# Second readings of the weights after attention: one landing tile or three, and how many pieces between two examinations

## The chip, the cores and the metric

The kernel runs on one core of one Trainium2 chip. The metric is device time in microseconds (us), the median of three runs, for the whole program: attention, the feed-forward block and all reading and writing of memory.

## The reference

Two computations follow each other. The first is a gated linear recurrence over 4 batches, 8 heads, 768 time steps and a head width of 48:

```python
for t in range(S):
    state = alpha[:, :, t, :, None] * state + np.einsum('bhd,bhe->bhde', k[:, :, t], v[:, :, t])
    y[:, :, t] = np.einsum('bhd,bhde->bhe', q[:, :, t], state)
```

The heads are then laid side by side (3072 tokens of width 384), and a feed-forward block is applied: `h = x @ w_in` (384 x 2048), `g = h * sigmoid(h)`, `out = g @ w_out` (2048 x 384). The weights come as 64-bit floats, everything else as 32-bit floats.

## The kernel before

Attention is cut into 24 chunks of 128 steps (one batch each), which go through the stages `products`, `quotient`, `scores`, `values` and `states`. From chunk 8 on, a chunk's alpha, k and q land in three fixed tiles, `late["quads"]` with the names a, k and q, each 128 x 800 floats. VectorE (DVE) turns them (`turned`), and each is free again once that has read it.

The feed-forward block works on groups of four chunks (six groups, `grp` 0 to 5). A group's first product goes into `g` tiles, and its second product goes out to memory. Both use fast-product schemes that trade matmuls for sums on DVE. They are written as Python generators, and one step of a generator is a *piece*. For a group from 2 on:

- `enter(grp, pair)` makes half of the hidden units in seven pieces, called E1 to E7 here. A piece has three products of two matmuls each (E7 has two products), into three PSUM banks `ps_m`; the profile records each matmul as two. ScalarE (ACT) copies a bank away or DVE adds or subtracts it (`tt`, recorded at line 944). DVE has one such step in each of E1 to E4, three in E5, four in E6, and three in E7, one of them recorded at L587. E7 also ends with two `side_by_side` sums (L1019). The activation (L941) is on ACT.
- `leave(grp, h)` makes the output for half a group's tokens in seven pieces, L1 to L7 here. Each is one product of eight matmuls (16 records) into one of the two banks `ps_o`, which `new(0)` and `new(1)` take. A line number with an L, such as L1042, is always four digits or three; L1 to L7 are pieces. L1 and L7 both take bank 0. L7's bank is emptied by DVE in `store` (line 1042), which also starts the write of the output. `subtract` (L1033) is DVE work, twice in each of L1, L3 and L4.

The list `pieces` fixes the order. After attention there are 41 pieces left: the rest of a *first block* (`leave(4,0)` and `enter(5,0)` in turn, L1 E1 L2 E2 ... L7 E7), a *second block* (`leave(4,1)` and `enter(5,1)`), and a *tail* (`leave(5,0)`, then `leave(5,1)`, L1 to L7 each with nothing between). `go_on()` issues the next piece.

The kernel is right only for inputs within certain bounds, and so it examines its inputs: the generator `audit()` reads alpha, w_in and w_out a second time, in 9, 12 and 16 transfers. DVE reduces each one, by one maximum for alpha and by a maximum and a minimum for the weights (line 685). Every transfer lands in the one tile `bits` of the pool `look`, so the next cannot start before the reduction is over. During attention's late steps `fill` takes a step of `audit()` every second slot. After attention a loop takes the remaining 17 steps, with one or two pieces after each in turn:

```python
    while next(audits, 0) is None:
        turns += 1
        for _ in range(1 + turns % 2):
            go_on()
```

After the loop DVE works out the flag: four reductions and comparisons (`ends`, `good`), five pieces, then one small matmul on TensorE (PE) and its comparison (`small`, line 1236), four pieces, then `values_load` (line 1239), with which each engine's sequencer reads the flag from memory. A hint for the branch at the program's end follows on each engine, then all pieces left. If the flag is zero a slower general version runs.

The framework's planner puts the instructions of each engine into one fixed order: by program order where inputs are ready by its own estimates, and with a later instruction ahead of an earlier one where they are not. `keep_in_program_order` ties an instruction behind the one traced just before it on its engine. It is used for every matmul in this phase and for the audit's reductions. It is not used for `tt`, `subtract` and `store`, nor for the flag's own steps. Each engine then runs its order strictly. The audit's transfers are issued by SyncE's queue (SP). So are the tail's outputs, while the outputs of earlier groups go by GpSimd's queue (POOL).

Of the kernel before, what the change touches and what calls it, by code (L numbers as in the profile page):

```python
# [8 lines left out]
F32 = mybir.dt.float32  # L9
I32 = mybir.dt.int32  # L10
# [345 lines left out]
def quotients(  # L356
# [19 lines left out]
    nc = tc.nc  # L376
    dve, act, gps = nc.vector, nc.scalar, nc.gpsimd

    late = {}
# [14 lines left out]
    B, H, S, D = q.shape  # L394
    C = 128
    NCH = S // C
    NP = H // 2
    HD = H * D
# [174 lines left out]
    quads = w_in.rearrange("p k (q i c) -> p i k q c", i=4, c=128)  # L573
# [83 lines left out]
    def audit():  # L657


        flat = alpha.rearrange("b h s d -> (b h s d)").rearrange("(p c) -> p c", p=128)  # L660
        todo = [(flat[:, c : c + AW], AW, 0) for c in range(0, flat.shape[1], AW)]
        if wide:
            todo += [(moe_w_in[t * 128 : t * 128 + 128, c : c + 512], 512, 1)
                     for c in range(0, DF, 512) for t in range(NKT)]
            todo += [(moe_w_out[f * 128 : f * 128 + 128, :], HD, 1) for f in range(NFT)]
        for kind in (0, 1):
            n = sum(x[2] == kind for x in todo)
            if n:
                seen.append([fix.tile([128, n], F32, name=f"seen{kind}{i}") for i in range(2)])
        at = [0, 0]  # L670
        for src, n, kind in todo:
            t = late["look"].tile([128, 512, 2], I32, name="bits")
            if kind == 0:
                x = t.rearrange("p n w -> p (n w)")[:, 0:n].bitcast(F32)
                nc.sync.dma_start(x, src)
            else:
                nc.sync.dma_start(t[:, 0:n, :].rearrange("p n w -> p (n w)"), src.bitcast(I32))
                x = t[:, 0:n, 1]
            yield
            i = at[kind]  # L680
            at[kind] += 1
            for which, op in ((0, ALU.max), (1, ALU.min)):
                if kind == 1 or which == 0:
                    tc.keep_in_program_order(
                        dve.tensor_reduce(seen[kind][which][:, i : i + 1], x, axis=AX, op=op,  # L685
                                          apply_absolute_value=True))
# [454 lines left out]
    def go_on():  # L1141

        nonlocal done
        next(pieces[done][0], None)
        done += 1

    audits = audit()
    done, bridged = 0, 0
    STEPS = NT + 1
# [4 lines left out]
    def settle():  # L1154

        first.close()
        late.update(look=pool("look"), part=pool("part"), xc=pool("xc"), turn=pool("turn"),
                    wx=pool("wx").tile([128, 8, NQ, 128], F32, name="wx"))
        quads = pool("quads")
        late["p"] = pool("p").tile([128, NP * W + 1], F32, name="p")  # L1160
        late["quads"] = {name: quads.tile([128, 32 + 4 * NP * D], F32, name=f"{name}t") for name in "akq"}
        for name, t in late["quads"].items():
            gps.memset(t, 1.0 if name == "a" else 0.0)
        load(NA)
# [20 lines left out]
    for step in range(STEPS):  # L1185
# [9 lines left out]
        for slot, group in enumerate(stages):  # L1195
            for stage, lag in group:
                n = step - lag
# [9 lines left out]
            if step * SLOTS + slot == (NA + 1) * SLOTS - 1:  # L1207
                x = decayed.rearrange("p (o i c) -> p o i c", o=2, c=C)
# [2 lines left out]
            fill(step, slot)  # L1211
            if step * SLOTS + slot >= NA * SLOTS - 1 and conv_done[1] == NFT and not late:
                settle()
    turns = 0
    while next(audits, 0) is None:
        turns += 1
        for _ in range(1 + turns % 2):
            go_on()

    checks = [(least.rearrange("p n j -> p (n j)"), ALU.min, 2.0**-64, ALU.is_gt),  # L1220
              (seen[0][0], ALU.max, 1.0, ALU.is_le)]
# [27 lines left out]
@with_exitstack  # L1249
def kernel(  # L1250
    ctx: ExitStack,
    tc: tile.TileContext,
    q: bass.AP,
    k: bass.AP,
    v: bass.AP,
    alpha: bass.AP,
    moe_w_in: bass.AP,
    moe_w_out: bass.AP,
    out: bass.AP,
):  # L1260


    flag = ctx.enter_context(tc.tile_pool(name="flag", bufs=1))
    small = flag.tile([1, 1], I32, name="small")
    args = (q, k, v, alpha, moe_w_in, moe_w_out, out)
    within = quotients(tc, small, *args)
    with tc.If(within < 1, label="general"):
        general(tc, *args)
# [30 lines left out]
```

## Time and profile before

| What | Value |
| --- | --- |
| median of 3 runs | 561.12 us (560.93 to 561.14) |
| span of the profiled execution, first to last instruction | 558.1 us |
| around the span, median less span | 3.0 us |
| PE busy | 541.4 us (97%) |
| DVE busy | 445.1 us (80%) |
| ACT busy | 208.4 us (37%) |
| POOL busy | 75.9 us (14%) |
| mean granted TensorE clock | 0.994 |
| DVE, line 685 (the audit): busy, idle before it | 42.5 us, 24.0 us |
| matmul pieces of attention end at about | 443 us |
| audit transfers of w_out issued | 454.2 to 514.8 us |

The profiled execution's own time is not listed apart from its span; the 3.0 us around it are what the runs have beyond the span. A group of instructions is one row: busy time, mean length of one in nanoseconds, and the idle time of its engine just before, with what ended it. Starts in a timeline are in us from the start of the span, and the second figure is the length of the row's instructions together. Ends of matmuls are modelled, so distances between starts are the safer measure on PE.

### The profile page before, as it was taken

What the parts mean: (1) busy time and instruction counts of PE and PEld (TensorE: products, weight loads), DVE (VectorE), ACT (ScalarE), POOL (GpSimd) and SP (SyncE); (2) the same over time, 40 slices, a digit from 0 to 9 for tenths busy, and PEclk for the clock granted to TensorE, in tenths of its full rate; (3) what the DMA queues carried; (4) which work ended last, traced back from release to release, by engine and by line L of the source; (5) the groups of instructions that cost most, each with busy time, mean ns of one, the idle gap of its engine ahead of it and who ended that gap; (6) DMA issues with size and microseconds to landing.
All of it is one profiled execution on the core that took longest, in us unless ns stands there. A gap on an engine that the chain in (4) does not pass through costs nothing. (4 is left out here: it accounts for less than half of the span.)

```text
span 558.1 us, 12640 instructions
## 1 busy us (share of the span) xinstructions
PE 541.4 (97%) x5026; PEld 488.8 (88%) x5026; DVE 445.1 (80%) x801; ACT 208.4 (37%) x466; POOL 75.9 (14%) x146
## 2 busy tenths in 40 slices
PE   5999999999999999999999999999999999999996
PEld 3788887998899898899999999988998999998996
DVE  5887889974999799997998986998894775857531
ACT  3456643223333243353353353353263341432200
POOL 4100010221211211021021021021121000001000
PEclk9799999999999999999999999999999999999999
DMA  9999861164445525355445654717712122333101
GB/s 218 255 276 177 232 189 40 38 164 108 126 131 136 142 62 134 88 145 157 129 109 142 194 141 115 198 22 179 180 48 84 53 99 95 111 109 106 38 25 32
DMA packets 99220, 70.13 MB, mean 126 GB/s; under 512 B 56272, under 2 KB 88656, under 8 KB 99152
## 3 DMA queue, kind: packets, MB, share of 16 engines
q1 hardware_dynamic: 97232, 65.30, 44.6%
q0 software_dynamic: 1920, 3.93, 2.0%
q8 instruction: 41, 0.67, 0.5%
q14 instruction: 27, 0.22, 0.1%
HBM read 61.34 MB, written 7.86 MB: 124 GB/s over the span
## 5 line engine op out<-in xcount | busy, mean ns | idle before, releaser
L388 PE MATMUL ps_o<-w_out,g 128*128 128x192 f32 x768 | 134.7, 329 | 1.1 <-DVE o L1042 0.9
L388 PEld LDWEIGHTS ps_o<-w_out,g 128*128 128x128 f32 x768 | 125.4, 190 | 5.1 <-DVE o L1042 2.3
L388 PE MATMUL ps_m<-xt,w_in 128*128 128x256 f32 x480 | 113.6, 383 | 1.5 <-ACT xt L851 1.1
L388 PEld LDWEIGHTS ps_m<-xt,w_in 128*128 128x128 f32 x480 | 89.1, 190 | 14.4 <-ACT xt L851 1.6
L388 PE MATMUL ps_o<-wt,g 128*128 128x192 f32 x576 | 99.7, 326 | 0.0
L388 PEld LDWEIGHTS ps_o<-wt,g 128*128 128x128 f32 x576 | 95.1, 190 | 1.6 <-issue 0.2
L388 PE MATMUL ps_m<-xc,w_in 128*128 128x256 f32 x288 | 70.7, 382 | 0.0
L685 DVE TENSOR_REDUCE seen<-bits 128x1 f32<-128x384 int32 (+2 forms) x65 | 42.5, 689 | 24.0 <-DMA bits<-in_moe_w_out_dram 19.6
L388 PEld LDWEIGHTS ps_m<-xc,w_in 128*128 128x128 f32 x288 | 53.6, 190 | 7.0 <-DVE g L944 0.3
L941 ACT ACTIVATE g<-g 128x1024 f32<-128x1024 f32 x32 | 33.0, 1056 | 59.0 <-DVE g L944 59.0
L1033 DVE TENSOR_TENSOR g<-g 128x512 f32<-128x512 f32 x72 | 49.8, 708 | 6.1 <-PE ps_o L388 6.1
L1045 POOL DMA_DIRECT2D out_dram<-o x40 | 22.0, 550 | 223.2 <-DVE o L1042 127.6
L813 POOL TENSOR_SCALAR_AFFINE_SELECT g<-g 64x256 f32<-64x256 f32 x64 | 34.2, 534 | 124.8 <-ACT g L806 105.8
L388 PE MATMUL ps_m<-xc,wx 128*128 128x256 f32 x192 | 50.0, 383 | 1.0 <-DVE xc L586 1.0
L936 ACT COPY g<-ps_m 128x512 f32<-128x512 f32 x64 | 36.5, 588 | 36.5 <-PE ps_m L388 36.4
L388 PEld LDWEIGHTS ps_m<-xc,wx 128*128 128x128 f32 x192 | 35.2, 190 | 5.3 <-ACT u L1064 1.3
L944 DVE TENSOR_TENSOR g<-ps_m,g 128x512 f32<-128x512 f32 x56 | 37.0, 684 | 2.9 <-PE ps_m L388 2.7
L722 DVE TENSOR_TENSOR_SCAN u<-al,one 128x516 f32<-128x516 f32 x24 | 30.0, 1249 | 10.6 <-ACT al L719 10.3
L909 ACT ACTIVATE g<-ps_m 128x512 f32<-128x512 f32 x32 | 19.1, 596 | 42.8 <-PE ps_m L388 42.3
L936 ACT COPY part<-ps_m 128x512 f32<-128x512 f32 x32 | 18.9, 589 | 43.0 <-DVE g L944 21.3
L752 DVE TENSOR_TENSOR_SCAN p<-al,inv 128x516 f32<-128x516 f32 x24 | 29.9, 1246 | 1.0 <-PE ps_a L388 0.4
L388 PE MATMUL ps_a<-g,vn 128*32 128x128 f32 x768 | 27.5, 278 | 1.8 <-POOL g L801 1.7
(126 smaller groups left out, 611.4 us busy)
## 6 DMA issues: line engine op xcount, KB each, us to landing
bits<-in_moe_w_in_dram SPq DMA_DIRECT2D x24, 512.0 KB, 4.8
bits<-in_moe_w_out_dram SPq DMA_DIRECT2D x32, 384.0 KB, 3.1
at<-in_alpha_dram SPq DMA_DIRECT2D x64, 96.0 KB, 2.5
kt<-in_k_dram SPq DMA_DIRECT2D x64, 96.0 KB, 2.5
qt<-in_q_dram SPq DMA_DIRECT2D x64, 96.0 KB, 2.6
bits<-in_alpha_dram SPq DMA_DIRECT2D x9, 512.0 KB, 3.8
out_dram<-o POOLq DMA_DIRECT2D x40, 96.0 KB, 2.4
flips<-turn SPq DMA_DIRECT2D x12, 256.0 KB, 2.4
```

What stands on the lines that cost most here:

```text
L388: in_order(nc.tensor.matmul(*args, **kw))
L685: dve.tensor_reduce(seen[kind][which][:, i : i + 1], x, axis=AX, op=op, apply_absolute_value=True))
L722: dve.tensor_tensor_scan(u[:, end - 1 :: -1], sg[:, end:0:-1], one[:, end:0:-1], 0.0, ALU.mult, ALU.add)
L752: dve.tensor_tensor_scan(p[:, 0:end], sg[:, 0:end], iv[:, 0:end], 0.0, ALU.mult, ALU.add)
L813: gps.affine_select(x, x, pattern=[[0, NP], [1, CH]], compare_op=ALU.is_ge, fill=0.0, base=0, channel_multiplier=-1)
L909: act.activation(gts[grp, h, pair][:, i : i + 2, q % 2, :], ps, AF.Silu)
L936: act.copy(to, ps)
L941: act.activation(x, x, AF.Silu)
L944: dve.tensor_tensor(to, a, b, op)
L1033: dve.tensor_tensor(cells(grp, h, pair, *to), cells(grp, h, pair, *x), cells(grp, h, pair, *y), ALU.subtract)
L1045: (gps if grp < NG - 1 else nc.sync).dma_start(out[r : r + C, c * HO : (c + 1) * HO], o)
```

## The change

`audit()` is split into a part that starts a transfer (`begin`) and a part that examines one. Transfers of alpha and w_in, 21 in all, still use the tile `bits`, one at a time. The 16 of w_out, which are 768 words wide, now land in the tiles a, k and q of attention in turn. From transfer number 20 on (counted from 0), up to two transfers beyond the one about to be examined are started. After attention the loop takes one piece per step of the audit, 17 in all, where it took two and one in turn, 26 in all. The flag's steps keep their distances of five and four pieces, and so they stand nine pieces earlier, as does all that follows them.

```diff
         flat = alpha.rearrange("b h s d -> (b h s d)").rearrange("(p c) -> p c", p=128)
+        assert 2 * HD <= 32 + 4 * NP * D
...
+        alone = sum(2 * x[1] > 32 + 4 * NP * D or x[2] == 0 for x in todo)
...
         at = [0, 0]
-        for src, n, kind in todo:
-            t = late["look"].tile([128, 512, 2], I32, name="bits")
+        landed = []
+
+        def begin(src, n, kind):
+            at = len(landed)
+            t = late["look"].tile([128, 512, 2], I32, name="bits").rearrange("p n w -> p (n w)") if (
+                at < alone) else late["quads"]["akq"[at % 3]].bitcast(I32)
             if kind == 0:
-                x = t.rearrange("p n w -> p (n w)")[:, 0:n].bitcast(F32)
-                nc.sync.dma_start(x, src)
+                landed.append(t[:, 0:n].bitcast(F32))
+                nc.sync.dma_start(landed[-1], src)
             else:
-                nc.sync.dma_start(t[:, 0:n, :].rearrange("p n w -> p (n w)"), src.bitcast(I32))
-                x = t[:, 0:n, 1]
+                nc.sync.dma_start(t[:, 0 : 2 * n], src.bitcast(I32))
+                landed.append(t[:, 0 : 2 * n].rearrange("p (n w) -> p n w", w=2)[:, :, 1])
+
+        for i, (src, n, kind) in enumerate(todo):
+
+            while len(landed) < min(i + (1 if i + 1 < alone else 3), len(todo)):
+                begin(*todo[len(landed)])
+            x = landed[i]
             yield
...
-    turns = 0
     while next(audits, 0) is None:
-        turns += 1
-        for _ in range(1 + turns % 2):
-            go_on()
+        go_on()
```

## The prediction

> **What bounds the kernel now.** I read the page's busy shares first (PE 97%), then the costliest groups for the audit, then PE's waits after attention, then the timelines around those waits. In the page's groups the audit is one row:
>
> ```profile
> L685 DVE TENSOR_REDUCE seen<-bits 128x1 f32<-128x384 int32 (+2 forms) x65 | 42.5, 689 | 24.0 <-DMA bits<-in_moe_w_out_dram 19.6
> ```
>
> DVE stood 24.0 us before reductions, 19.6 of them for transfers of w_out. That is no gain in itself. The waits that end on PE and on its weight loads (PEld) from 440 us on are few; these two lists hold all of substance:
>
> ```profile
> PE ps_o L388 <- DVE o L1042: 0.9, 2, 0.7
> ...
> PEld ps_o L388 <- DVE o L1042: 2.1, 3, 1.1
> PEld ps_a L388 <- issue: 0.6, 2, 0.3
> PEld ps_o L388 <- ACT g L941: 0.4, 1, 0.4
> ```
>
> So PE waits for `store` (L1042) and once for an activation. Where? The timeline of all engines at the end of the second block:
>
> ```profile
> 509.64 1.01 DVE L685 TENSOR_REDUCE seen<-bits 128x1 f32<-128x384 int32 x2 [0.91 <-DMA bits<-in_moe_w_out_dram]
> ...
> 510.48 2.76 PE L388 MATMUL ps_o<-wt,g 128*128 128x192 f32 x16
> ...
> 513.08 1.03 PE L388 MATMUL ps_m<-xc,w_in 128*128 128x256 f32 x4
> ...
> 513.75 1.00 DVE L685 TENSOR_REDUCE seen<-bits 128x1 f32<-128x384 int32 x2
> ...
> 513.94 1.03 PE L388 MATMUL ps_m<-xt,w_in 128*128 128x256 f32 x4
> 514.67 0.68 DVE L587 SCALAR_TENSOR_TENSOR g<-g 128x512 f32<-128x512 f32 x1
> 515.27 0.35 DVE L1042 TENSOR_TENSOR o<-ps_o,u 128x192 f32<-128x192 f32 x1
> ...
> 515.68 3.25 PE L388 MATMUL ps_o<-w_out,g 128*128 128x192 f32 x16 [0.71 <-DVE o L1042]
> ...
> 517.36 1.27 PEld L388 LDWEIGHTS ps_o<-w_out,g 128*128 128x128 f32 x8 [0.41 <-ACT g L941]
> ...
> 518.77 2.76 PE L388 MATMUL ps_o<-wt,g 128*128 128x192 f32 x16
> ```
>
> L7's product starts at 510.48 and is over at 513.08, but DVE, busy without a gap since 509.64 after 0.91 us lost to a transfer, comes to L7's `store` only at 515.27. The tail's L1 needs that bank.
>
> Undisturbed spacing: a four-record product takes 513.94 - 513.08 = 0.86, an L piece 2.60 (518.77 to 521.37, the next start). L1 was due at 513.94 + 0.87 = 514.81 and the piece behind it at 517.41, yet that starts at 518.77: **1.36 us lost** in the second block. The first block's end, from PE's own timeline:
>
> ```profile
> 477.27 1.03 PE L388 MATMUL ps_m<-xc,w_in 128*128 128x256 f32 x4
> 478.14 1.03 PE L388 MATMUL ps_m<-xt,w_in 128*128 128x256 f32 x4
> 479.24 2.87 PE L388 MATMUL ps_o<-w_out,g 128*128 128x192 f32 x16
> 481.94 1.89 PE L388 MATMUL ps_m<-xc,w_in 128*128 128x256 f32 x8
> ```
>
> The piece at 481.94 was due at 477.27 + 1.73 + 2.60 = 481.60: **0.34 us lost**. Everything else between 444 and 519 us runs at 2.60 a piece. What the change can win is thus 1.70 us.
>
> **The Trainium skill.** "PSUM — Partial Sum Buffer", Engine vs sequencer instructions: VectorE's queue is strictly first in, first out, and matmuls complete in program order. The trace agrees: at 515.27 `store` stood 2.2 us behind its product. "DMA: Bandwidth & Descriptors", Anatomy of one DMA: about 2.0 us fixed plus bytes / 436 GB/s, written for GpSimd's path; as an estimate 2.0 + 393,216 B / 436e3 = 2.9 us. SP's transfers of w_out show a median of 2.9 after 454 us, so it fits. "SBUF — State Buffer", Who interferes with whom: transfers don't contend with compute engines, nor `tensor_reduce` with GpSimd; I cost another landing place at nothing. "Runtime: NRT & Kernel Launch", Instruction fetch mechanics: a taken branch outside the fetched window waits for a fetch; no stall of that sort shows here.
>
> **The change, part by part.**
>
> *Same work.* 16 transfers and 65 reductions stay, at two reductions in 0.93 us of DVE (473.33 to 474.25 and its like).
>
> *Removed: waits for w_out on DVE.* A transfer is started when the examination three before it is over. At a piece (2.60) per step that is 7.8 us, less 0.93 for the examination itself, ahead of need; against 2.9 median, 7.1 the longest bits transfer in the trace. The 19.6 us of waits go. The first three of w_out may even be issued from about 412 us, as q's last turning starts at 410.52; 1.2 MB at a time when the transfers have gaps. At worst they delay a remaining w_in transfer by 1.2 MB / 200 GB/s = 6 us, when DVE is 2.85 of 10 us busy (420 to 430). I take zero, and 1 us as the upper end.
>
> *Added: density in the first block.* 17 examinations over 17 pieces in place of 26. The first block gets about 13 in 36.4 us (14 pieces), not 8 or 9. DVE's load there is 13 x 0.93 = 12.1, 0.6 more for two longer ones of w_in, 14 E-steps and two `side_by_side` at 0.60 = 9.6, six `subtract` 3.6, six short ones at 0.36 = 2.1, and the 11 sums of the group at 0.36 = 4.0: 32 of 36.4 us. It fits, on average. The tight place is E5 to E7, where one examination stands behind each piece. With PE at its present starts, and 0.21 us from a product's end to DVE (466.89 to 467.10 for `store` of L5):
>
> - L5's `store` 467.10, its examination to 468.4. E5's first sum when ACT has copied (468.55): 468.60, second to 469.80; ACT copies the third product by 470.3, last sum to 470.95.
> - examination to 471.88; L6 (product over 472.08): two short ones 472.29 to 472.95; examination to 473.88.
> - E6's four sums: 473.88 to 476.28 (its last product is over at 474.67); examination to 477.21.
> - E7's first sum, which needs no product (recorded L587), to 477.81; then L7's `store`, whose product is over at 477.27: done at 478.16.
>
> Before, it ended at 478.83 + 0.35 = 479.18. L1 is due at 479.00, so there are 0.84 us to spare. If ACT does its activation before the copy, the chain starts 1.2 us later and `store` is done at about 479.0, just in time. **-0.34**, or 0 at the worst of these.
>
> *Removed from the second block.* Step 17 falls behind its second E piece. From 490 us no examination is left, and E6 and E7 have DVE alone: L7's `store` runs at about 513.3 and E7's sum at 514.05 (product over 513.94), the activation of 1.06 us ends at 515.8, and L1's second half needs it at 514.81 + 1.30 = 516.1. Neither wait remains: **-1.36**. What is late next: nothing up to the tail's L7-L1 bank wait (0.18 at 535.36), which has no audit in it and stays.
>
> *Moved: the flag, nine pieces earlier.* About ten tiny DVE steps (0.13 to 0.17 each) fall where DVE now has nothing to examine. The flag's matmul cost 526.78 - 526.57 = 0.21 of PE and costs that again; its `good` is ready 12 us ahead. `values_load` (about 0.5 us on each engine's sequencer) and the hint move from 527 to about 503 us. On PE the load ran at 531.8 and the next matmul came 0.11 late (532.09 for 531.98). If the planner puts it directly behind the matmul, PE's sequencer waits 527.25 - 526.66 = 0.59 for `small`, then 0.53 for load and hint: 1.1. On DVE 0.54 us falls before E5 or E6 of the second block, where DVE has over 2 us to spare; ACT is idle from 504.3 to 507.4; behind POOL's load stand two output writes, behind SP's only the tail's. I take nothing beyond before's 0.11; ends 0 and +1.0. The branch at the end is now hinted 39 us ahead of it: if its fetch were lost, SP's branch at 554.4 has cover until the last output's signal at 556.4. Zero; a longer fetch would show at the end.
>
> Sum: 558.1 - 0.34 - 1.36 = 556.4 span; with the same 3.0 around it 561.12 - 1.70 = **559.4 us**.
>
> **Rivals.**
>
> *A: gain eaten, within 0.2%.* Either the flag's load blocks PE (1.1 - 0.11), which leaves 1.7 - 1.0 = 0.7: 560.4; or the examinations in E5 to E7 crowd `store` of the first block as the second was crowded, +1.36 there for -1.36 here: 561.1. For it: DVE is 88% full in that block and the planner's order is not known. Against: its 0.84 us to spare, and no examination there can wait for a transfer any more. Value 560.6.
>
> *B: slower; three tiles are not enough.* If landing takes T, three pieces take at least T + 0.33 issue + 0.93. At T = 2.9 that is 1.4 a piece, hidden. It reaches 2.60 at T = 6.5. With 7.1 us throughout, 2.79 a piece: 13 x 0.19 = 2.4 lost in the first block against 1.36 won: 562.2; that is where "slower by over 0.2%" begins. Were the transfers to run strictly one at a time, each step would take its present 4.0 us (513.75 less 509.64 is 4.1): 13 x 1.4 = 18 us lost, 578. For it: SP waits in order, and one late examination holds all transfers behind. Against: the medians, and the engines' transfers are 30% busy.
>
> *C: the change doesn't do what it says.* If the planner kept waits as they are, 17 waits in 17 pieces is the 578 above; counted with B.
>
> **How the numbers follow.** A measurement of this kernel tells about 0.2%, 1.12 us, from no change. Likeliest case 0.62: 559.4, own range 558.9 to 560.0, all faster. Rival A 0.20: same. B and other losses 0.18: slower. The range runs from 558.9 to 561.9: the likeliest and A hold 0.82; the early transfers' 1 us and the flag's 1.0 lie in it.
>
> **What would show it.** Right: no idle time of DVE before L685 ended by w_out; examinations over by about 490 us; L1 of both blocks' ends at 2.60 spacing, PE's waits for L1042 down from 0.9 to about 0.2. Wrong: w_out waits remain (B), L1042 in the first block later than 478.6 or a PE gap beside the flag's load (A), or time after the last output's write.

## The result, and the profile after

| Kernel | Median, us | Range | Runs |
| --- | --- | --- | --- |
| before, in this comparison | 560.54 | 559.08 to 561.23 | 13 |
| changed | 558.43 | 557.46 to 559.85 | 13 |

The ratio is 0.9963, with a 95% interval of 0.9951 to 0.9974: **2.1 us faster**, between 1.5 and 2.7. The forecast was 559.4 us with a range from 558.9, so the direction was right and the time lies half a microsecond below the range. The profiled execution has a span of 556.1 us where the working had 556.4; how much of this nearness is luck is told under the measure below.

The audit's row in the page's groups now holds only the 33 reductions of alpha and w_in, where it held 65:

```profile
L697 DVE TENSOR_REDUCE seen<-bits 128x1 f32<-128x512 int32 (+1 forms) x33 | 26.3, 823 | 6.0 <-DMA bits<-in_moe_w_in_dram 6.0
```

The list of waits of the changed kernel from 437 us on (microseconds in total, number of waits, longest) has these rows for PE, PEld and the audit:

```profile
PEld ps_o L388 <- DVE o L1054: 0.8, 1, 0.8
...
DVE seen L697 <- DMA qt<-in_moe_w_out_dram: 0.7, 2, 0.6
DVE seen L697 <- DMA bits<-in_moe_w_in_dram: 0.7, 1, 0.7
PEld ps_a L388 <- issue: 0.6, 2, 0.3
PE ps_o L388 <- DVE o L1054: 0.5, 1, 0.5
PEld ps_o L388 <- issue: 0.2, 1, 0.2
```

DVE's wait for w_out has gone from 19.6 to 0.7 us. PE waits for `store` (now L1054) once and not twice, and no longer for an activation. That one wait has grown, though: it was 0.18 us before and is 0.51 now. This is the end of the second block in the changed kernel's timeline of all engines (start, length, engine, operation, idle time before it):

```profile
509.26 2.76 PE L388 MATMUL ps_o<-wt,g 128*128 128x192 f32 x16
510.27 0.68 DVE L587 SCALAR_TENSOR_TENSOR g<-g 128x512 f32<-128x512 f32 x1
...
511.86 1.03 PE L388 MATMUL ps_m<-xc,w_in 128*128 128x256 f32 x4
512.06 0.36 DVE L1054 TENSOR_TENSOR o<-ps_o,u 128x192 f32<-128x192 f32 x1 [1.11 <-PE ps_o L388]
...
512.73 1.03 PE L388 MATMUL ps_m<-xt,w_in 128*128 128x256 f32 x4
...
513.59 2.76 PE L388 MATMUL ps_o<-w_out,g 128*128 128x192 f32 x16
513.65 2.01 ACT L953 ACTIVATE g<-g 128x1024 f32<-128x1024 f32 x2 [2.21 <-DVE g L956]
...
516.19 0.98 PE L388 MATMUL ps_o<-wt,g 128*128 128x192 f32 x5
```

`store` runs 0.20 us after its product is over (511.86), and DVE had been waiting for it 1.11 us. Before, it ran 2.2 us after. L1 follows at 513.59, 0.86 after the product before it, and the next piece 2.60 after that: no loss is left here. Two things went at once in this block: the waits for transfers, and the examinations themselves, which are over by now. `tiles_only` below goes some way to part them. The end of the first block:

```profile
476.08 1.03 PE L388 MATMUL ps_m<-xc,w_in 128*128 128x256 f32 x4
...
476.59 0.35 DVE L1054 TENSOR_TENSOR o<-ps_o,u 128x192 f32<-128x192 f32 x1
...
477.80 2.76 PE L388 MATMUL ps_o<-w_out,g 128*128 128x192 f32 x16
...
480.40 1.89 PE L388 MATMUL ps_m<-xc,w_in 128*128 128x256 f32 x8
```

From E7 to the piece behind L1 it is 480.40 - 476.08 = 4.32 us, where it was 481.94 - 477.27 = 4.67.

**A measure for what follows.** The profiles of one kernel differ by more than the effect looked for. The first block's L1 starts anywhere from 441.7 to 443.7 us in the 14 profiles of this study, whatever the kernel. The *distance* from that start to the start of the last L7 leaves out both what comes before and how long the last output takes to land. These are the two starts, first of the kernel before and then of the changed kernel:

```profile
443.43 2.87 PE L388 MATMUL ps_o<-w_out,g 128*128 128x192 f32 x16
...
550.73 2.76 PE L388 MATMUL ps_o<-wt,g 128*128 128x192 f32 x16
```

```profile
442.23 2.87 PE L388 MATMUL ps_o<-w_out,g 128*128 128x192 f32 x16
...
548.16 2.76 PE L388 MATMUL ps_o<-wt,g 128*128 128x192 f32 x16
```

It is 550.73 - 443.43 = 107.30 us before, and 548.16 - 442.23 = 105.93 changed: **1.37 us shorter**. The spans differ by 558.1 - 556.1 = 2.0: the first block starts 1.20 us earlier in the changed kernel's profile, 1.37 are in the distance, and the end, after the last L7's start, is 0.57 longer (7.94 for 7.37). Neither the start nor the end can be laid to the change: over the 14 profiles the end, too, lies anywhere from 7.37 to 8.57. So the span came near the working's partly by luck.

### The profile page after: what moved, and what is told of

Read it like the earlier page. It is cut to its first block, busy times and chain, and to the rows that moved or that the text cites. A ratio compares the mean times of both kernels' runs of the same rounds, so it can differ in the third digit from the quotient of the medians.

```text
span 556.1 us, 12642 instructions
## 1 busy us (share of the span) xinstructions
PE 539.2 (97%) x5026; PEld 488.0 (88%) x5026; DVE 446.0 (80%) x801; ACT 208.4 (37%) x466; POOL 75.7 (14%) x146
## 5 line engine op out<-in xcount | busy, mean ns | idle before, releaser
L697 DVE TENSOR_REDUCE seen<-bits 128x1 f32<-128x512 int32 (+1 forms) x33 | 26.3, 823 | 6.0 <-DMA bits<-in_moe_w_in_dram 6.0
L1054 DVE TENSOR_TENSOR o<-ps_o,u 128x192 f32<-128x192 f32 x24 | 8.5, 353 | 25.0 <-PE ps_o L388 22.1
```

Of the source, the lines that this page charges most:

```text
L1054: dve.tensor_tensor(o, x, y, ALU.add)
```

## The experiments

Each was run in the same session as the kernel before, which had medians of 558.88 to 559.11 us there.

**One landing tile, one piece per examination** (`loop_only`): half of the change alone.

```diff
-    turns = 0
     while next(audits, 0) is None:
-        turns += 1
-        for _ in range(1 + turns % 2):
-            go_on()
+        go_on()
```

> The kernel before with the loop alone changed: one piece per examination, still one landing tile, so the flag stands nine pieces earlier but every transfer still waits for the examination before it. Theory (the landing tiles are what pays; a single tile keeps the 4.0 us cycle): 17 examinations end about 518 us as before, the flag's matmul stands on PE behind the fifth piece of the second block (over at 502.7 us), so PE waits there about 17 us; the two stalls at the blocks' ends may go: 561 + 17 - 1.4, about 576 us. Rival (the earlier end of the examinations in program order is enough, the planner spreads them): 559 to 561 us.

Measured: 576.24 us, ratio 1.0314 (1.0289 to 1.0338), distance 566.00 - 441.71 = 124.29. From its timeline of all engines:

```profile
503.99 1.01 DVE L685 TENSOR_REDUCE seen<-bits 128x1 f32<-128x384 int32 x2 [2.35 <-DMA bits<-in_moe_w_out_dram]
507.91 1.01 DVE L685 TENSOR_REDUCE seen<-bits 128x1 f32<-128x384 int32 x2 [2.91 <-DMA bits<-in_moe_w_out_dram]
511.75 1.01 DVE L685 TENSOR_REDUCE seen<-bits 128x1 f32<-128x384 int32 x2 [2.83 <-DMA bits<-in_moe_w_out_dram]
515.81 1.01 DVE L685 TENSOR_REDUCE seen<-bits 128x1 f32<-128x384 int32 x2 [3.05 <-DMA bits<-in_moe_w_out_dram]
...
517.47 0.19 PE L388 MATMUL ps_a<-ones,good 128*1 128x1 f32 x2 [16.23 <-DVE good L1228]
```

The expectation was met. With one tile an examination takes 4 us in either loop, and PE, whose order has the flag's matmul behind L5, waits 16.2 us for the last of them. The tiles of attention are what lets the flag stand early: with them the examinations keep pace with the pieces.

**Three landing tiles, the old loop** (`tiles_only`): the other half alone.

```diff
-    while next(audits, 0) is None:
-        go_on()
+    turns = 0
+    while next(audits, 0) is None:
+        turns += 1
+        for _ in range(1 + turns % 2):
+            go_on()
```

> The changed kernel with the old loop, two pieces and one in turn: three landing tiles, but examinations last until the end of the second block, and the flag stays where it was. Measure: distance on PE from the start of the first block's L1 to the start of the last L7 (107.30 us before, 105.93 changed). Theory (waits for transfers made DVE late, not the number of examinations): no wait of DVE for w_out, the loss of 0.34 in the first block gone, the second block's L1 starts on time, its activation up to 0.3 late as one examination stands between L7's store and E7's sum: about 105.9, as good as the changed kernel, 558.5 to 559. Rival (an examination in E6 and E7 is what hurts, waiting or not): the second block keeps most of its 1.36 us loss: about 107.0, some 560 us.

Measured: 557.88 us, ratio 0.9977 (0.9969 to 0.9984), distance 548.51 - 442.52 = 105.99. The distance came out as the theory had it, with its small remainder: no wait for w_out is left, PE's waits for `store` are 0.2 us, and an activation is late, as before the change:

```profile
PEld ps_o L388 <- DVE o L1054: 0.5, 1, 0.5
...
PEld ps_o L388 <- ACT g L953: 0.4, 1, 0.4
...
PE ps_o L388 <- DVE o L1054: 0.2, 1, 0.2
```

So the tiles alone bring 1.31 of the 1.37 us. What one piece per step adds is seen in the next experiment.

That the waits were the cause, and not the examinations as such, is shown for the first block alone. There an examination still stands between E6's sums and E7's first one (at 474.8 us), as it did before, and the loss is gone all the same. In the second block the planner also placed DVE's work differently:

```profile
510.83 0.68 DVE L587 SCALAR_TENSOR_TENSOR g<-g 128x512 f32<-128x512 f32 x1
...
512.03 0.36 DVE L1054 TENSOR_TENSOR o<-ps_o,u 128x192 f32<-128x192 f32 x1 [0.53 <-PE ps_o L388]
512.30 1.00 DVE L697 TENSOR_REDUCE seen<-at 128x1 f32<-128x384 int32 x2
```

Before, an examination stood between E6's sums and L587 with `store` behind it (513.75). Here none does, and one comes right behind `store`. An estimate from the lines of before says that the wait alone would have done nearly as much: the last transfer's 0.91 us delayed `store` to 515.27, and L1 started 0.41 after that. Without the 0.91, in the old order, L1 would have started at about 514.36 + 0.41 = 514.77, on time (514.81), with the late activation left. No run tests this by itself.

**The flag at its old place** (`flag_late`).

```diff
     while next(audits, 0) is None:
         go_on()
+    for _ in range(9):
+        go_on()
```

> The changed kernel with nine more pieces between the last examination and the flag's steps, so that the flag stands where it stood before. Theory (before, the reading of the flag between the two outputs of the tail let the planner draw the first matmul of L2 ahead of L1 into the wait for L7's bank; the changed kernel lost that): L7 to L1 in the tail 2.94 and not 3.27 us apart counted to the next but one piece, the distance from the first L1 to the last L7 105.6 against 105.93, 0.3 us faster than the changed kernel (too little for the timed runs to tell apart). Rival (the 0.33 us come from the flag's matmul in the second block and nothing in the tail differs): the distance stays 105.9.

Measured: 557.38 us, ratio 0.9969 (0.9957 to 0.9981), distance 548.93 - 443.33 = 105.60, as the theory said. Against `tiles_only`, whose flag stands at the same place, the one piece per step brings 105.99 - 105.60 = 0.39 us: the late activation is gone. Moving the flag then costs 105.93 - 105.60 = 0.33, so that the new loop as a whole gains 0.06. Its PE timeline in the tail, and the same place in the changed kernel:

```profile
530.28 3.09 PE L388 MATMUL ps_o<-wt,g 128*128 128x192 f32 x18
533.55 2.87 PE L388 MATMUL ps_o<-w_out,g 128*128 128x192 f32 x16 [0.18 <-DVE o L1054]
536.26 2.44 PE L388 MATMUL ps_o<-wt,g 128*128 128x192 f32 x14
538.53 1.79 PE L388 MATMUL ps_o<-w_out,g 128*128 128x192 f32 x10
```

```profile
529.19 2.76 PE L388 MATMUL ps_o<-wt,g 128*128 128x192 f32 x16
532.46 2.87 PE L388 MATMUL ps_o<-w_out,g 128*128 128x192 f32 x16 [0.51 <-DVE o L1054]
535.16 2.76 PE L388 MATMUL ps_o<-wt,g 128*128 128x192 f32 x16
537.76 2.44 PE L388 MATMUL ps_o<-w_out,g 128*128 128x192 f32 x14
```

In the first, 18 records stand in L7's row and 14 in L2's: L2's first matmul (two records) has slipped in front of L1, and fills PE's wait for L7's bank. From L7 to L3 it is 538.53 - 530.28 = 8.25 us there and 537.76 - 529.19 = 8.57 here. In the kernel before it is the same (18, 16 and 14 records), and in the changed kernel, whose flag stands elsewhere, it is not. That the flag's place decides this is thus shown; how it does so is read from the code. In program order the reading of the flag comes between L1 and L2, and `keep_in_program_order` ties a matmul only to what was traced just before it on PE. L2's first matmul is tied to the flag's reading and not to L1, and the planner may draw it forward. No trace shows the planner's reasons.

**The two output banks exchanged in every second output** (`banks`, and again as `banks_again`): a trial of a better version.

```diff
         def new(i):
-            return out_bank(i, HO)
+            return out_bank(i ^ h, HO)
```

> The changed kernel with the two output banks exchanged in every second output (the first product of one output no longer takes the bank of the last product of the one before). Theory (what still stops PE in the tail is the one shared bank, 3.27 us from L7 to L1 for 2.60): 0.67 us off, distance from the first L1 to the last L7 about 105.3, some 557.8 us where the changed kernel has 558.4. Rival (PE is held there by the flag or by the queue): no change of the 3.27.

Measured: 557.35 us, ratio 0.9968 (0.9956 to 0.9980), distance 547.26 - 442.11 = 105.15. L7 and L1 are now 2.60 us apart in PE's rows, and none of its waits for `store` is left:

```profile
529.06 2.76 PE L388 MATMUL ps_o<-wt,g 128*128 128x192 f32 x16
531.66 2.76 PE L388 MATMUL ps_o<-w_out,g 128*128 128x192 f32 x16
```

> The kernel with the output banks exchanged once more, beside the changed kernel on one chip. Theory: distance 105.15 as before, timed 0.5 to 1.1 us faster than the changed kernel in this comparison. Rival (what PE saves is lost at the end in the last output's landing): no difference between the two.

Measured: 557.37 us, ratio 0.9964 (0.9950 to 0.9978), distance 548.49 - 443.34 = 105.15, and 0.83 us faster than the changed kernel's 558.20 in the same session. This version is faster than both kernels. Beside `flag_late`, whose distance is 0.45 longer, its times show no difference (557.35 and 557.38 in one session, with 8 and 9 runs).

**Both kernels a second time, and the changed kernel a third.**

> The kernel before, unchanged, for a second profile. Theory (the 1.2 us that the changed kernel's trace is ahead at the start of the first block, and the 0.6 us that it is behind after the last store, are differences between executions): the first block's L1 starts between 442 and 444 us, the time from the last store's start to the end of the span varies by half a microsecond, while the distance from the first L1 to the last L7 is 107.3 within 0.1. Rival (the change itself moves the early part or the end): 443.4 and 4.5 us again.

Measured: 559.32 us, ratio to the kernel before 1.0008 (0.9997 to 1.0020), distance 549.01 - 442.17 = 106.84. The start of the first block moved, as expected. The distance did not stay, which it had been expected to do: it is 0.46 shorter than in the first profile, and the part at the second block's end is 0.9 us and not 1.36. There the waits for w_out add up to 19.0 us and not 19.6. What the kernel before loses differs between executions.

> The changed kernel, unchanged, for a second profile. Theory as for the second profile of the kernel before: distance from the first L1 to the last L7 105.93 within 0.1, the start of the first block and the end differ from the first profile by up to 1.5 and 0.6 us; timed, 1.5 to 2.5 us faster than before. Rival (a systematic early gain): the first block starts at 442.2 again.

> The changed kernel once more, for the size of its gain: the distance is 105.93 again; timed against before the two comparisons so far gave 0.9963 and 0.9985, and if the kernel before is what varies, this one lies between 0.995 and 0.999.

Measured: 558.11 us, ratio 0.9985 (0.9977 to 0.9992), and 558.20 us, ratio 0.9979 (0.9971 to 0.9987); distances 549.16 - 443.23 = 105.93 and 549.60 - 443.68 = 105.92. The changed kernel's distance is the same in all three profiles. The gain in time was 2.1 us in the first comparison, and by the ratios 0.8 and 1.2 in these, where the second comparison had been expected to show 1.5 to 2.5. The distances explain 0.9 to 1.4 of it. The difference between the comparisons lies mostly with the kernel before: its median was 560.54 us in the first and 558.88 to 559.32 later, the changed kernel's 558.43 and then 558.11 and 558.20. Why the kernel before took longer there, some 0.7 us or more beyond the distances, is seen in no trace and stays open.

**Two landing tiles, one transfer ahead** (`two_tiles`).

```diff
-                at < alone) else late["quads"]["akq"[at % 3]].bitcast(I32)
+                at < alone) else late["quads"]["ak"[at % 2]].bitcast(I32)
...
-            while len(landed) < min(i + (1 if i + 1 < alone else 3), len(todo)):
+            while len(landed) < min(i + (1 if i + 1 < alone else 2), len(todo)):
```

> The changed kernel with two landing tiles and one transfer ahead. Theory (a cycle of two pieces is 5.2 us, and landing 2.9, issue 0.33 and examination 0.93 make 4.2): waits for w_out on DVE stay under 2 us in all and PE's distance from the first L1 to the last L7 stays at 105.9 to 106.2. Rival (two ahead is needed): DVE waits of 5 us or more, examinations end later, distance 106.5 or more.

Measured: 557.80 us, ratio 0.9982 (0.9973 to 0.9990), distance 549.56 - 443.63 = 105.93. DVE's waits for w_out are 1.9 us in four places, none of which reaches PE. One transfer ahead is enough for this distance.

**No second reading of w_out** (`no_w_out`): 16 transfers and 32 reductions left out.

```diff
-            todo += [(moe_w_out[f * 128 : f * 128 + 128, :], HD, 1) for f in range(NFT)]
...
-    while next(audits, 0) is None:
-        go_on()
+    for _ in range(NFT + 1):
+        next(audits, 0)
+        go_on()
```

> The changed kernel without the second reading of w_out (16 transfers and 32 reductions left out, so w_out's bounds are not examined), the pieces and the flag where the changed kernel has them. Theory (the audit costs PE nothing any more): distance from the first L1 to the last L7 105.9, the changed kernel's, timed the same within 0.2%. Rival (16 us of reductions still delay PE somewhere): shorter by more than 0.3 us.

Measured: 558.53 us, ratio 0.9993 (0.9983 to 1.0003), distance 547.64 - 441.71 = 105.93. Within this distance the audit of w_out costs PE nothing any more. The runs are no faster than the changed kernel's 558.11 in the same session; the two ratios' intervals overlap. In this profile the span ends 8.56 us after the last L7's start, against 7.94 in the changed kernel's first, and nothing in the trace says why.

**Every late transfer of w_out twice** (`before_twice`, `after_twice`): to make landings later.

```diff
+                if n == HD and at[1] > 14:
+                    e = late["quads"]["k"].bitcast(I32)
+                    tc.keep_in_program_order(nc.sync.dma_start(e[:, 0 : 2 * n], src.bitcast(I32)))
                 nc.sync.dma_start(t[:, 0:n, :].rearrange("p n w -> p (n w)"), src.bitcast(I32))
```

The edit shown is that of `before_twice`. In `after_twice` the second transfer goes into the tile `bits`, started beside the last 13 transfers.

> The kernel before with a second transfer of the same 384 KB of w_out into a free tile, started beside each of the last 13 transfers of the audit, so that these land later; DVE's order of instructions is that of the kernel before. Theory (what the kernel before loses at the blocks' ends grows with the landing time, 1.70 us in the first profile and 1.23 in the second): DVE waits for w_out 8 us or more above the 19 to 20 us, distance on PE from the first L1 to the last L7 above 108.5 us (107.30 and 106.84 without). Rival (the loss comes from the number of reductions alone): 106.8 to 107.3.

Measured: 561.11 us, ratio 1.0032 (1.0021 to 1.0044), distance 551.13 - 443.58 = 107.55. The expectation was missed because the means failed: the audit's own transfers landed in 3.0 us where they take 2.9, and DVE waited 20.2 us for them. It does not tell theory and rival apart. The time is 2.0 us longer than that of the kernel before, most of it outside the distance and unexplained.

> The changed kernel with the same 13 second transfers, into the tile that the audit of w_in has left. Theory (three tiles take the landing time off the path): distance 105.9 to 106.1, as without. Rival (landing later reaches DVE again, as two ahead is a short lead): DVE waits for w_out of 5 us or more and a distance over 106.5.

Measured: 559.22 us, ratio 1.0003 (0.9991 to 1.0015), distance 548.09 - 442.16 = 105.93. Here the audit's transfers did land later, at medians of 3.7 to 4.2 us against 3.2 to 3.3, and DVE waited 2.4 us once. PE's distance did not move. Timed, it is about 1 us slower than the changed kernel, outside the distance.

## Why the prediction was right or wrong

**The waits and where they go: right.** The first block's L7 `store` was worked out to end at 478.16 us. It ended at 476.59 + 0.35 = 476.94 in a profile whose first block starts 1.20 us earlier, so at 478.14 by the old clock. At the first block's end 4.67 - 4.32 = 0.35 us were won for 0.34 foretold. In the second block, from L7 to the tail's second product, 516.19 - 509.26 = 6.93 stand against 518.77 - 510.48 = 8.29: 1.36 won for 1.36 foretold. The examinations end at 490.5 us (491.7 by the old clock), foretold about 490. So close a match is in part owed to taking the same profile of before that the working was made from; against its second profile the second block wins 0.9 us. The three early transfers, put at nothing, cost nothing that shows: they started at 402.8, 404.4 and 412.1 us, and from the feed-forward block's first matmul to the first block's L1 it is 419.1 to 419.5 us in the changed kernel's three profiles and 419.2 and 419.3 in those of before.

**The flag moved at no cost: wrong by 0.33 us.** The step says that its matmul costs 0.21 and its reading 0.11 at the new place as at the old. The sum is right and the reading's share is not: both parts belong to the matmul. These are the flag's matmul and what follows it, before and changed:

```profile
526.66 0.19 PE L388 MATMUL ps_a<-ones,good 128*1 128x1 f32 x2
526.78 5.47 PE L388 MATMUL ps_o<-w_out,g 128*128 128x192 f32 x32
532.09 3.09 PE L388 MATMUL ps_o<-wt,g 128*128 128x192 f32 x18
```

```profile
501.26 0.19 PE L388 MATMUL ps_a<-ones,good 128*1 128x1 f32 x2
501.38 1.13 PE L388 MATMUL ps_m<-xc,wx 128*128 128x256 f32 x4
502.35 1.03 PE L388 MATMUL ps_m<-xt,wx 128*128 128x256 f32 x4
```

In both, the product right behind it takes 0.11 us more than its like: 502.35 - 501.38 = 0.97 for 0.86, and 532.09 - 526.78 = 5.31 for two pieces of 2.60. In the trace of before they are lost at 527.05, the second start behind the flag's matmul (0.27 us after the first, where 0.16 is usual), and PE's sequencer did the reading only at 531.8. In the changed kernel L5 to L6 takes 504.07 - 498.56 = 5.51 where a pair takes 5.19, and the reading, at 508.9, is not among it.

What the working had wrong is the tail. It held that the wait for L7's bank "stays" as it was. It had not asked why it was only 0.18 us. The flag's place had let one matmul of L2 into it, and with the flag gone the wait is 0.51, and the distance is 0.33 longer than that of `flag_late`. Sum: 0.35 + 1.36 - 0.33 = 1.38, and the distances say 1.37.

**The conversion from span to time: wrong by about 1.3 us, and this took the time out of the range.** The step that failed is "the same 3.0 around it", which is also the row "around the span" in the table of before: the median of three runs, 561.12, less the span of another execution. In every run that lists both, the time is 1.7 to 1.9 us more than its own span (557.79 and 556.1 for the changed kernel's profiled run). By that gap the profile before was of an execution of about 559.8 us, not of the 561.12 that it was set against. The working's span, 556.4, with 1.75 gives 558.15, 0.3 from the median measured.

That nearness has luck in it too, since the profiled execution was itself some 0.7 us faster than the median of thirteen, 560.54. Set against that median, the miss of 1.0 us (559.4 for 558.43) is 0.6 from a start that was too high (561.12 for 560.54) and 0.4 from a gain of 2.1 where 1.70 was forecast; the distances do not show this 0.4. The likeliest case's own range was also too narrow, 1.1 us, when thirteen executions of the kernel before alone cover 2.2.

**Rivals.** A did not happen: PE's sequencer read the flag at 508.9 us, in 0.5 us, and the products around it keep their 0.86 and 2.60 us (508.40, 509.26, 511.86), so it blocked nothing; and the first block's `store` was over 0.86 us before L1 was due. B did not happen with three tiles, nor with two. Its strict form, one transfer at a time at 4 us, was made in `loop_only`: 17.0 us lost by the distance (124.29 less 107.30), 18 worked out, at the flag's matmul and not piece by piece as B had it. The planner had let the pieces' DVE work pass the waiting examinations: four of these still came after 503 us, when PE had gone through all pieces ahead of the flag's matmul.

## What to carry to other kernels

A buffer that an earlier phase has left can turn a strict cycle of transfer and use into one with a lead, and what this is worth is read at the few places where the waiting engine is late for the one that bounds the kernel, not from the waiting time: 19 us of waits cost PE 1.2 to 1.7 us. A wait that stays short before a change should be asked why it is short; something moved may have been filling it. And a span is turned into a time with the gap between an execution's own two numbers, never with another execution's.

## What was not expected of the hardware

The same start differs in two clusters. The first matmul of the feed-forward block began at 22.7 to 23.0 us in six of the 14 profiles and at 23.5 to 24.3 in eight, with both kernels in both clusters (22.84 and 24.27 before; 22.82, 24.17 and 24.19 changed). Most of the offset stays: the first two profiles compared here differ by 1.45 us at that matmul and still by 1.20 at the first block's L1, nearly as much as the change itself. Two profiles alone would have shown it as part of the gain. What makes the two clusters is open.
